# Float64 weights: low words rounded on ScalarE and added as integers, two early units instead of three

## The chip, the cores and the metric

The kernel runs on one core of one Trainium2 chip. The metric is the device time of one execution in microseconds (us), as the median of several runs. A profile of one execution, with its trace, is there beside the times.

## The reference

```python
def _moe2_ref(x, w_in, w_out):          # x: 1152 tokens x 512; w_in 512 x 2048; w_out 2048 x 512
    h = x @ w_in
    relu6 = np.clip(h + 3.0, 0.0, 6.0)
    g = h * relu6 / 6.0
    return (g @ w_out).astype(np.float32)

def reference(...):
    attn_out = _attn_ref(q, k, v)       # windowed attention, 2 x 8 heads x 576 x 64
    x = attn_out -> (1152, 512)
    x = _moe_ref(x, w_gate, w1, w2, capacity)   # top-1 of 8 experts, 512 -> 1024 -> 512
    return _moe2_ref(x, w_in, w_out)    # the dense layer
```

`w_in` and `w_out` are made by dividing a float32 array by a float64 scalar and arrive as float64. The kernel reads them as pairs of 32-bit words, a low and a high one for each number, and has to make float32 of them itself. All else is float32.

## The kernel before, in words

The work has three parts in time: the attention with the routing (to about 80 us), the experts (to about 220 us), and the dense layer. TensorE (PE) multiplies in float32r, with each operand split into a rounded high part and a remainder; a product is three passes (`PASSES`). Splitting a piece of weights of 128x512 takes a ScalarE (ACT) copy at L269 and a VectorE (DVE) subtract at L274, both into a tile named `wt`.

Weights come in units of 256 columns of the hidden dimension. The 32 units of the experts are numbered 0 to 31, the 8 units of the dense layer 32 to 39; a unit has two halves (up and down weights) and four pieces. The halves pass through a ring of 6 raw tiles (`raw`) and a ring of 8 split tiles (`wt`). The dense layer's token groups are 640, 512, then 384 and 256 again; the first group runs over dense units 0 to 3 in eight steps of 128 columns, the second over all eight units. In step f, PE makes the up products (L255 `banks<-x,wt`), then the down products of the step before (L255 `banks<-wt,g`); between them ACT and DVE make the activation: L1558 `r` on ACT, L1561 `gf` on DVE, L1564 `g` on ACT, L1567 `g` on DVE.

A piece of the float64 weights is converted by `conv64`: a load of 128x1024 words into one of three tiles `raw64`; the absolute value of the high word on ACT (L208) into a tile `c64`; then on DVE a clamp (L212), a mask with a shift (L216), a join with the sign (L223), the power of two of the result (L229), the low word multiplied by it (L232), and the add (L238). Tiles `c64` and `t64` have two buffers each.

Dense units 0 to 2 (`NSC = 3`) are converted early, while the experts run: their loads go out on the GpSimd (POOL) queue, their results go from `t64` to DRAM (L241, `wd_dram`) on the same queue, and are loaded back into a raw tile (L1136) on it when the unit is due. Units 3 to 7 are converted straight into their raw tile; their loads go out on the SyncE (SP) queue, after the last load of expert weights.

The order on each engine is written by a planner when the program is built. Jobs (a load, a conversion, a split) are lists of operations with assumed costs for each engine; `fill` puts into the gaps of the engines what fits, in the order of a due time, and `need` forces whatever a unit still lacks. Early conversions have a late due time (`m + ZDUE`, three units after their own), conversions into the raw tile an early one (`m - AHEAD[1]`, 1.5 units before), splits that of their unit. `Ring` keeps when buffers come free in the planner's time. Engines work in the order of the program: an operation that waits holds up all behind it on its engine.

Of the kernel before, what the change touches and what calls it, by code (L numbers as in the profile page):

```python
# [9 lines left out]
F32 = mybir.dt.float32  # L10
# [4 lines left out]
U32 = mybir.dt.uint32  # L15
AF = mybir.ActivationFunctionType
# [7 lines left out]
def tile_kernel(ctx, tc, q, k, v, w_gate, w1, w2, w_in, w_out, out, cap):  # L24
    nc = tc.nc
# [149 lines left out]
    NDU = DFF // FU  # L175
    UW = 2 * NC * FU
    HW = UW // 4
    NSC = 3
    cv = ctx.enter_context(tc.tile_pool(name="cv", bufs=2))
    wd_dram = [dram.tile([128, UW], F32, name=f"wd_dram{u}") for u in range(NSC)]  # L180
    w_in32 = w_in.bitcast(U32)
    w_out32 = w_out.bitcast(U32)
    TINY = 2.0 ** -15
    HUGE = 131071.9921875

    def conv64(u, i, dst):

        box = {}  # L190

        queue = nc.gpsimd if u < NSC else nc.sync

        def load():
            box["raw"] = raw = cv.tile([128, 2 * HW], U32, name="raw64", bufs=NR64)
            if i < 2:
                src = w_in32[256 * i : 256 * i + 256, 2 * FU * u : 2 * FU * u + 2 * FU]
                queue.dma_start(raw.rearrange("p (c f) -> p c f", c=2), src.rearrange("(c p) f -> p c f", p=128))
            else:
                r0 = FU * u + 128 * (i - 2)  # L200
                queue.dma_start(raw, w_out32[r0 : r0 + 128, :])
            w = raw.rearrange("p (n t) -> p n t", t=2)
            box["lo"], box["hi"] = w[:, :, 0], w[:, :, 1]

        def c_abs():
            box["c"] = cv.tile([128, HW], U32, name="c64", bufs=NC64)
            box["t"] = cv.tile([128, HW], F32, name="t64", bufs=NC64)
            nc.scalar.activation(box["c"].bitcast(F32), box["hi"].bitcast(F32), AF.Abs)  # L208

        def c_clamp():  # L210
            c = box["c"].bitcast(F32)
            nc.vector.tensor_scalar(out=c, in0=c, scalar1=TINY, scalar2=HUGE, op0=ALU.max, op1=ALU.min)  # L212

        def c_shift():
            c = box["c"]
            nc.vector.tensor_scalar(  # L216
                out=c, in0=c, scalar1=0x07FFFFFF, scalar2=3, op0=ALU.bitwise_and, op1=ALU.logical_shift_left
            )

        def a_join():  # L220
            d = dst()
            box["a"] = a = box["hi"].bitcast(F32) if d is None else d
            nc.vector.scalar_tensor_tensor(  # L223
                out=a.bitcast(U32), in0=box["hi"], scalar=0xC0000000, in1=box["c"],
                op0=ALU.bitwise_and, op1=ALU.bitwise_or,
            )

        def c_power():
            nc.vector.tensor_single_scalar(box["c"], box["a"].bitcast(U32), 0xFF800000, op=ALU.bitwise_and)  # L229

        def t_low():
            nc.vector.scalar_tensor_tensor(  # L232
                out=box["t"], in0=box["lo"], scalar=2.0 ** -52, in1=box["c"].bitcast(F32), op0=ALU.mult, op1=ALU.mult
            )

        def t_add():
            a, t = box["a"], box["t"]
            nc.vector.tensor_tensor(out=a if u >= NSC else t, in0=a, in1=t, op=ALU.add)  # L238

        def store():  # L240
            nc.gpsimd.dma_start(wd_dram[u][:, HW * i : HW * i + HW], box["t"])  # L241

        return load, c_abs, c_clamp, c_shift, a_join, c_power, t_low, t_add, store

    NR64, NC64 = 3, 2

# [80 lines left out]
    with ExitStack() as actx:  # L329
# [514 lines left out]
        def early_relu(u):  # L844
            def run(e):
                if "hfE" not in box:
                    box["hfE"] = cv.tile([128, HW], F32, name="t64", bufs=NC64)
                    box["hE"] = cv.tile([128, HW], F32, name="t64", bufs=NC64)
                if e == "A":
                    nc.scalar.activation(box["hfE"][:, early_part(u)], box["uE", u], AF.Relu)  # L850
                else:
                    V.tensor_scalar_max(box["hfE"][:, early_part(u)], box["uE", u], 0.0)

            return run
# [245 lines left out]
            self.rel.append(None)  # L1100
            return len(self.rel) - 1

    r_raw, r_wt, r_64, r_ct = Ring(2 * NRAW), Ring(2 * NWT), Ring(NR64), Ring(NC64)

    def whole(m):

# [42 lines left out]
    def conv_job(u, i, m=None):  # L1149
        h = i // 2  # L1150
        ix = {}

        def dst():
            return None if m is None else raw_t[m, h][:, HW * (i % 2) : HW * (i % 2) + HW]

        load, c_abs, *mid, t_add, store = conv64(u, i, dst)

        def gate_load():
            a = 0.0 if m is None or (m, h) in raw_t else r_raw.free(raw_at[m, h])
            b = r_64.free()  # L1160
            return None if a is None or b is None else max(a - 2.0, b)

        def run_load(e, fin):
            if m is not None and (m, h) not in raw_t:
                take_raw(m, h)
            ix["raw"] = r_64.take()
            load()
            return (fin if m is not None else spend("D", 1.46, fin)) + 2.0

        def run_abs(e, fin):  # L1170
            ix["ct"] = r_ct.take()
            c_abs()
            return fin

        def plain(fn):
            def run(e, fin):
                fn()
                return fin + 0.13

            return run  # L1180

        def run_add(e, fin):
            t_add()
            r_64.rel[ix["raw"]] = fin
            if m is not None:
                r_ct.rel[ix["ct"]] = fin
                raw_ready[m, i] = fin + 0.2
            return fin + 0.2

        def run_store(e, fin):  # L1190
            store()
            r_ct.rel[ix["ct"]] = fin + 2.0
            stored[u, h] = stored.get((u, h), 0) + 1
            return fin

        now = lambda: 0.0
        ops = [({"D": 1.46} if m is not None else {"P": 1.1}, gate_load, run_load), ({"A": 0.6}, r_ct.free, run_abs)]
        ops += [({"V": c}, now, plain(fn)) for c, fn in zip((0.34, 0.4, 0.62, 0.34, 0.62), mid)]
        ops.append(({"V": 0.62}, now, run_add))
        return ops + ([({"P": 1.1}, now, run_store)] if m is None else [])  # L1200

    def split_job(m, i):
# [468 lines left out]
    def dense_again():  # L1671

        for t0 in range(0, NTOK, 512):
            n = min(512, NTOK - t0)
            acc = [bank("acc") for _ in range(n // 128)]
            for u in range(DFF // FU):
                halves = [wk.tile([128, 2, NC, 256], F32R, name="xT256", bufs=XTB) for _ in range(2)]
                halves = [x.rearrange("p a c f -> p a (c f)") for x in halves]
                for i in range(NPC):
                    r = wk.tile([128, HW], F32, name="xg", bufs=3)  # L1680
                    if u < NSC:
                        nc.sync.dma_start(r, wd_dram[u][:, HW * i : HW * i + HW])
                    else:
                        load, c_abs, *mid, t_add, _ = conv64(u, i, lambda: r)
                        for fn in (load, c_abs, *mid, t_add):
                            fn()
                    high, low = split_ops(halves[i // 2], r, i % 2)
                    high("A")
                    low()
                for b in range(2):  # L1690
                    ph = bank("rot")[:, 0:n]
                    up = [
                        (w_up(halves, wi, c, 128 * b, 128), x2[:, xi, c, t0 : t0 + n]) for wi, xi in PASSES for c in range(NC)
                    ]
                    mm(ph, up)
                    r = wk.tile([128, 512], F32, name="y", bufs=1)[:, 0:n]
                    gf = wk.tile([128, 2, 256], F32R, name="h", bufs=4).rearrange("p a n -> p (a n)").bitcast(F32)[:, 0:n]
                    g = wk.tile([128, 2, NC, 128], F32R, name="xT128", bufs=XTB).rearrange("p a c t -> p a (c t)")[:, :, 0:n]
                    nc.scalar.activation(r, ph, AF.Relu, bias=c_three)
                    V.scalar_tensor_tensor(out=gf, in0=r, scalar=6.0, in1=ph, op0=ALU.min, op1=ALU.mult)  # L1700
                    nc.scalar.copy(g[:, 0], gf)
                    V.tensor_tensor(out=g[:, 1], in0=gf, in1=g[:, 0].bitcast(F32), op=ALU.subtract)
                    for i in range(n // 128):
                        mm(
                            acc[i],
                            [(g[:, gi, 128 * i : 128 * i + 128], w_dn(halves, wi, b, 0, DM)) for wi, gi in PASSES],
                            start=(u == b == 0), stop=(u == DFF // FU - 1 and b == 1),
                        )
# [165 lines left out]

    est.update(clock)
    est["D"] = max(est["D"], done["rk"] + 1.7)
    for ring, t in ((r_64, est["P"]), (r_ct, done["g0"] + 4.0)):
        ring.rel = [t] * ring.n
    for _ in range(NFIRST):
        assert advance(lambda j, e, t, c: e == "D")  # L1880
# [111 lines left out]
```

## Time and profile before

| what | value |
|---|---|
| median of 3 runs | 438.41 us (437.16 to 441.8) |
| the profiled execution | 438.62 us |
| its span, first to last instruction | 436.9 us |
| mean granted TensorE clock | 0.987 |
| busy in the span | PE 407.5 us, DVE 320.4 us, ACT 225.0 us, POOL 68.2 us |
| chain that ended last, by engine | PE 57%, DVE 20%, DMA 9%, issue 8%, ACT 3% |

Busy time of PE counts matmuls that overlap, so that a stall of PE is read from the starts of its matmuls. The chain is followed back from the last instruction, at each step to what released it.

### The profile page before, as it was taken

The numbers are of one execution on the slowest core, as the hardware profiler recorded it, in microseconds if no ns is written. First come the engines' busy times: TensorE is split into PE (matmuls) and PEld (weight loads), VectorE is DVE, ScalarE is ACT, GpSimd is POOL, SyncE is SP. The second block draws the span as 40 slices with busy tenths as digits, with TensorE's granted clock in tenths as the row PEclk, the third lists the DMA queues.
The fourth block names the chain that finished last, engine by engine and source line by source line (L and its number), as shares of the span: only waits on it lengthen the run. The fifth ranks groups of instructions, "written<-read, shape, count | busy, mean of one in ns | idle before, by whom it ended". The sixth has DMA issues, their size and how long they took to land.

```text
span 436.9 us, 8572 instructions
## 1 busy us (share of the span) xinstructions
PE 407.5 (93%) x3055; PEld 345.8 (79%) x3055; DVE 320.4 (73%) x864; ACT 225.0 (51%) x495; POOL 68.2 (16%) x138
## 2 busy tenths in 40 slices
PE   7999887899999999999999887999999999999990
PEld 4887665597889998978989776888888888999980
DVE  2888967688999999799874899999999323322530
ACT  4786864564668876464761653465554222322320
POOL 8533405024020020212200000000000000200200
PEclk9999999999999999999999998999999999999996
DMA  9997957989999998789914333442410000100110
GB/s 174 202 224 179 302 206 253 362 263 373 372 345 315 312 364 244 251 288 347 344 62 115 94 105 96 146 106 88 145 50 0 1 0 2 72 24 1 53 47 28
DMA packets 68114, 75.98 MB, mean 174 GB/s; under 512 B 31104, under 2 KB 49536, under 8 KB 68064
## 3 DMA queue, kind: packets, MB, share of 16 engines
q1 hardware_dynamic: 62928, 57.70, 43.7%
q0 software_dynamic: 5136, 17.67, 11.4%
q8 instruction: 26, 0.43, 0.4%
q14 instruction: 24, 0.20, 0.1%
HBM read 67.49 MB, written 7.86 MB: 172 GB/s over the span
## 4 chain that ended last, share of the span: by engine, by line
PE 57%; DVE 20%; DMA 9%; issue 8%; ACT 3%; SPq 1%; POOL 0%; POOLq 0%; DVEq 0%; ACTq 0%
PE banks L255 48%; DVE wt L274 7%; DMA raw<-in_moe_w_dram 4%; PE banks L512 2%; PE banks L630 2%; DMA c<-x_dram,sidx 1%; DVE neg L589 1%; DMA v_sb<-in_v_dram 1%; PE banks L1472 1%; PE banks L612 1%; DMA wd_dram<-t 1%; DVE t L232 1%; DVE raw L223 1%; PE banks L576 1%; SPq L480 1%
## 5 line engine op out<-in xcount | busy, mean ns | idle before, releaser
L255 PE MATMUL banks<-x,wt 128*128 128x320 f32 (+3 forms) x576 | 108.6, 340 | 2.5 <-DVE wt L274 2.2
L255 PEld LDWEIGHTS banks<-x,wt 128*128 128x128 f32 x576 | 95.7, 191 | 12.8 <-DVE wt L274 2.7
L255 PE MATMUL banks<-wt,g 128*128 128x512 f32 x384 | 93.9, 392 | 2.9 <-ACT g L1564 1.4
L255 PEld LDWEIGHTS banks<-wt,g 128*128 128x128 f32 x384 | 71.4, 188 | 18.4 <-DVE wt L274 2.1
L274 DVE TENSOR_TENSOR wt<-raw,wt 128x512 fp32r<-128x512 f32 x128 | 82.5, 682 | 3.4 <-ACT wt L269 3.3
L269 ACT CAST wt<-raw 128x512 fp32r<-128x512 f32 x128 | 74.1, 622 | 19.4 <-DMA raw<-wd_dram 7.3
L1561 DVE SCALAR_TENSOR_TENSOR gf<-r,banks 128x320 f32<-128x320 f32 (+3 forms) x48 | 26.5, 552 | 55.1 <-ACT r L1558 55.1
L1558 ACT ACTIVATE r<-banks,c_three 128x320 f32<-128x320 f32 (+3 forms) x48 | 27.9, 580 | 63.8 <-PE banks L255 63.8
L255 PE MATMUL banks<-xT,wt 128*128 128x256 f32 (+2 forms) x288 | 38.7, 283 | 1.0 <-ACT hf L1428 0.7
L255 PEld LDWEIGHTS banks<-xT,wt 128*128 128x128 f32 x288 | 35.0, 191 | 3.1 <-DVE wt L274 0.8
L255 PE MATMUL banks<-h,wt 128*128 128x256 f32 (+2 forms) x288 | 37.0, 279 | 0.0
L255 PEld LDWEIGHTS banks<-h,wt 128*128 128x128 f32 x288 | 34.6, 192 | 0.5 <-issue 0.5
L1564 ACT CAST g<-gf 128x320 fp32r<-128x320 f32 (+2 forms) x40 | 21.4, 536 | 25.4 <-DVE gf L1561 25.3
L208 ACT ACTIVATE c<-raw 128x512 f32<-128x512 f32 x32 | 21.6, 674 | 16.4 <-DVE t L232 13.2
L1567 DVE TENSOR_TENSOR g<-gf,g 128x320 fp32r<-128x320 f32 (+2 forms) x40 | 23.3, 582 | 8.2 <-ACT g L1564 8.1
L1604 POOL DMA_INDIRECT out_dram<-raw,cidx x4 | 4.0, 988 | 142.5 <-ACT raw L1601 134.9
L255 PE MATMUL banks<-wt,xT 128*128 128x256 f32 x144 | 21.6, 293 | 1.3 <-DVE wt L274 0.8
L589 DVE CUSTOM_DVE_ANT_0 neg<-banks,tmask 128x128 f32<-128x128 f32 x72 | 16.2, 284 | 8.8 <-PE banks L576 8.8
L232 DVE SCALAR_TENSOR_TENSOR t<-raw,c 128x512 f32<-128x512 uint32 x32 | 22.0, 688 | 0.6
L602 ACT ACTIVATE pe<-neg,nmx 128x128 f32<-128x128 f32 x72 | 22.3, 392 | 0.1
L223 DVE SCALAR_TENSOR_TENSOR raw<-raw,c 128x512 uint32<-128x512 uint32 x32 | 22.0, 687 | 0.5
L255 PEld LDWEIGHTS banks<-wt,xT 128*128 128x128 f32 x144 | 18.6, 190 | 3.9 <-DVE wt L274 2.3
(288 smaller groups left out, 573.9 us busy)
## 6 DMA issues: line engine op xcount, KB each, us to landing
raw<-in_moe_w_dram SPq DMA_DIRECT2D x64, 512.0 KB, 6.3
raw<-in_moe_w_in_dram SPq DMA_DIRECT2D x10, 512.0 KB, 3.8
raw<-in_moe_w_out_dram SPq DMA_DIRECT2D x10, 512.0 KB, 3.7
early<-in_moe_w_dram SPq DMA_DIRECT2D x8, 512.0 KB, 7.3
raw<-in_moe_w_in_dram POOLq DMA_DIRECT2D x6, 512.0 KB, 7.2
raw<-in_moe_w_out_dram POOLq DMA_DIRECT2D x6, 512.0 KB, 7.0
wd_dram<-t POOLq DMA_DIRECT2D x12, 256.0 KB, 5.9
raw<-wd_dram POOLq DMA_DIRECT2D x6, 512.0 KB, 6.8
```

The costliest lines, as they stand in the source:

```text
L208: nc.scalar.activation(box["c"].bitcast(F32), box["hi"].bitcast(F32), AF.Abs)
L223: nc.vector.scalar_tensor_tensor(out=a.bitcast(U32), in0=box["hi"], scalar=0xC0000000, in1=box["c"], op0=ALU.bitwise_and, op1=ALU.bitwise_or,)
L232: nc.vector.scalar_tensor_tensor(out=box["t"], in0=box["lo"], scalar=2.0 ** -52, in1=box["c"].bitcast(F32), op0=ALU.mult, op1=ALU.mult)
L255: nc.tensor.matmul(out, l, r, start=(start and n == 0), stop=(stop and n == len(pairs) - 1))
L269: nc.scalar.copy(hi, r)
L274: V.tensor_tensor(out=lo, in0=r, in1=hi.bitcast(F32), op=ALU.subtract)
L589: V.tensor_tensor_reduce(out=neg[:, hp, :], in0=box["sp", g][:, hp, :], in1=tmask[:, first, :], scale=-1.0, scalar=3.0e38, op0=ALU.add, op ...
L602: nc.scalar.activation(pe[:, hp, :], neg[:, hp, :], AF.Exp, bias=nmx[:, hp : hp + 1], scale=-1.0)
L1558: nc.scalar.activation(r, ph, AF.Relu, bias=c_three)
L1561: V.scalar_tensor_tensor(out=gf, in0=r, scalar=6.0, in1=ph, op0=ALU.min, op1=ALU.mult)
L1564: nc.scalar.copy(hi, gf)
L1567: V.tensor_tensor(out=lo, in0=gf, in1=hi.bitcast(F32), op=ALU.subtract)
```

## The change

Per piece, ACT gets a second operation: the low word, an unsigned integer, is multiplied by 2^-29 and written back in place as a rounded integer (0 to 8). DVE then joins clamp, shift and sign into `c64` and adds the two words as 32-bit integers: the power of two (L229) and the multiplication of the low word (L232) are gone, and the add has integer operands. The tile `t64` is taken only by the add of an early piece, with a ring of its own, and the planner counts it free 5 us after the store's issue instead of 2. `NSC` goes from 3 to 2, so that dense unit 2 is converted straight into its raw tile. The upper limit of the clamp and the planner's costs change with it.

```diff
-    NSC = 3
+    NSC = 2
...
-    HUGE = 131071.9921875
+    HUGE = 122880.0
...
         def c_abs():
             box["c"] = cv.tile([128, HW], U32, name="c64", bufs=NC64)
-            box["t"] = cv.tile([128, HW], F32, name="t64", bufs=NC64)
             nc.scalar.activation(box["c"].bitcast(F32), box["hi"].bitcast(F32), AF.Abs)
+
+        def c_round():
+            nc.scalar.activation(box["lo"], box["lo"], AF.Copy, scale=2.0 ** -29)
...
         def a_join():
-            d = dst()
-            box["a"] = a = box["hi"].bitcast(F32) if d is None else d
             nc.vector.scalar_tensor_tensor(
-                out=a.bitcast(U32), in0=box["hi"], scalar=0xC0000000, in1=box["c"],
+                out=box["c"], in0=box["hi"], scalar=0xC0000000, in1=box["c"],
                 op0=ALU.bitwise_and, op1=ALU.bitwise_or,
             )
 
-        def c_power():
-            nc.vector.tensor_single_scalar(box["c"], box["a"].bitcast(U32), 0xFF800000, op=ALU.bitwise_and)
-
-        def t_low():
-            nc.vector.scalar_tensor_tensor(
-                out=box["t"], in0=box["lo"], scalar=2.0 ** -52, in1=box["c"].bitcast(F32), op0=ALU.mult, op1=ALU.mult
-            )
-
         def t_add():
-            a, t = box["a"], box["t"]
-            nc.vector.tensor_tensor(out=a if u >= NSC else t, in0=a, in1=t, op=ALU.add)
+            d = dst()
+            if d is None:
+                box["t"] = d = cv.tile([128, HW], F32, name="t64", bufs=NT64)
+            nc.vector.tensor_tensor(out=d.bitcast(U32), in0=box["c"], in1=box["lo"], op=ALU.add)
...
+    NR64, NC64, NT64 = 3, 2, 2
...
         def run_add(e, fin):
+            if m is None:
+                ix["t"] = r_t.take()
             t_add()
-            r_64.rel[ix["raw"]] = fin
+            r_64.rel[ix["raw"]] = r_ct.rel[ix["ct"]] = fin
...
         def run_store(e, fin):
             store()
-            r_ct.rel[ix["ct"]] = fin + 2.0
+            r_t.rel[ix["t"]] = fin + 5.0
...
-        ops += [({"V": c}, now, plain(fn)) for c, fn in zip((0.34, 0.4, 0.62, 0.34, 0.62), mid)]
-        ops.append(({"V": 0.62}, now, run_add))
+        ops.append(({"A": 0.57}, now, plain(c_round)))
+        ops += [({"V": c}, now, plain(fn)) for c, fn in zip((0.34, 0.34, 0.61), mid)]
+        ops.append(({"V": 0.61}, now if m is not None else r_t.free, run_add))
```

## Rows read from the trace of the kernel before

**Rows 1.** Stretches: length, busy us (x count) by engine; TensorE clock, DMA share, GB/s.

```profile
core 0: us, PE busy (x) PEld busy (x) DVE busy (x) ACT busy (x) POOL busy (x), PEclk, DMA share, GB/s
...
134.00:166.00 32.00, 31.23 (x253) 29.92 (x252) 31.26 (x70) 24.60 (x54) 3.70 (x3) 1.00 0.99 332
...
220.00:280.00 60.00, 54.86 (x295) 48.71 (x296) 49.22 (x101) 26.37 (x51) 1.09 (x2) 0.97 0.31 94
280.00:300.00 20.00, 20.00 (x90) 16.57 (x89) 19.59 (x37) 10.58 (x18) 0.00 (x0) 1.00 0.37 107
```

**Rows 2.** The chain that ended last: start, us, what.

```profile
276.83 149.89 PE banks L255 x725
```

**Rows 3.** PE in order of time: start, us, what [idle before <- releaser].

```profile
230.33 3.68 PE L255 MATMUL banks<-x,wt 128*128 128x320 f32 x24
...
237.27 3.68 PE L255 MATMUL banks<-x,wt 128*128 128x320 f32 x24
...
246.30 3.68 PE L255 MATMUL banks<-x,wt 128*128 128x320 f32 x24
...
253.24 3.68 PE L255 MATMUL banks<-x,wt 128*128 128x320 f32 x24
...
261.70 0.74 PE L255 MATMUL banks<-x,wt 128*128 128x320 f32 x4
264.63 4.88 PE L255 MATMUL banks<-x,wt 128*128 128x320 f32 x20 [2.19 <-DVE wt L274]
...
272.77 3.68 PE L255 MATMUL banks<-x,wt 128*128 128x320 f32 x24
...
280.13 2.88 PE L255 MATMUL banks<-x,wt 128*128 128x512 f32 x12
```

**Rows 4.** Waits of PE from 205 to 285: total us, times, longest.

```profile
PE banks L255 <- DVE wt L274: 3.4, 2, 2.2
PE banks L255 <- ACT g L1564: 1.4, 1, 1.4
```

**Rows 5.** The chain, 214 to 242.

```profile
215.50 16.53 issue
232.04 4.67 DMA wd_dram<-t
...
237.23 3.91 DMA raw<-wd_dram
```

**Rows 6.** DVE in order of time.

```profile
231.05 0.69 DVE L238 TENSOR_TENSOR t<-raw,t 128x512 f32<-128x512 f32 x1
...
242.25 0.49 DVE L1561 SCALAR_TENSOR_TENSOR gf<-r,banks 128x320 f32<-128x320 f32 x1 [6.88 <-ACT r L1558]
...
257.66 1.28 DVE L274 TENSOR_TENSOR wt<-raw,wt 128x512 fp32r<-128x512 f32 x2
```

**Rows 7.** Groups by line: count, busy us, mean ns, idle before.

```profile
L232 DVE SCALAR_TENSOR_TENSOR t<-raw,c 128x512 f32<-128x512 uint32 x32 | 22.0, 688 | 0.6
L223 DVE SCALAR_TENSOR_TENSOR raw<-raw,c 128x512 uint32<-128x512 uint32 x32 | 22.0, 687 | 0.5
...
L208 ACT ACTIVATE c<-raw 128x512 f32<-128x512 f32 x32 | 21.6, 674 | 16.4 <-DVE t L232 13.2 <-PE banks L1405 1.3 <-DMA raw<-in_moe_w_out_dram 1.0
...
L238 DVE TENSOR_TENSOR raw<-raw,t 128x512 f32<-128x512 f32 x20 | 13.8, 688 | 0.3
L229 DVE TENSOR_SCALAR c<-raw 128x512 uint32<-128x512 uint32 x32 | 13.7, 429 | 0.6
...
L216 DVE TENSOR_SCALAR c<-c 128x512 uint32<-128x512 uint32 x32 | 13.6, 425 | 0.3
...
L212 DVE TENSOR_SCALAR c<-c 128x512 f32<-128x512 f32 x32 | 13.4, 420 | 2.0 <-ACT c L208 1.9
```

**Rows 8.** Waits of PE from 85 to 205.

```profile
PE banks L255 <- DVE wt L274: 1.0, 4, 0.3
...
PE banks L1308 <- DVE xg L1300: 0.6, 1, 0.6
```

**Rows 9.** Stores to `wd_dram`, L241: us from issue to landing.

```profile
DMA to landing us min/median/max: 2.9/5.9/8.4
```

More of the change, by code (lines that the diff above doesn't have):

```diff
@@ L220, in a_join @@
         def a_join():
-            d = dst()
-            box["a"] = a = box["hi"].bitcast(F32) if d is None else d
             nc.vector.scalar_tensor_tensor(
-                out=a.bitcast(U32), in0=box["hi"], scalar=0xC0000000, in1=box["c"],
+                out=box["c"], in0=box["hi"], scalar=0xC0000000, in1=box["c"],
                 op0=ALU.bitwise_and, op1=ALU.bitwise_or,
             )
-        def c_power():
-            nc.vector.tensor_single_scalar(box["c"], box["a"].bitcast(U32), 0xFF800000, op=ALU.bitwise_and)
-        def t_low():
-            nc.vector.scalar_tensor_tensor(
-                out=box["t"], in0=box["lo"], scalar=2.0 ** -52, in1=box["c"].bitcast(F32), op0=ALU.mult, op1=ALU.mult
-            )
         def t_add():
-            a, t = box["a"], box["t"]
-            nc.vector.tensor_tensor(out=a if u >= NSC else t, in0=a, in1=t, op=ALU.add)
+            d = dst()
+            if d is None:
+                box["t"] = d = cv.tile([128, HW], F32, name="t64", bufs=NT64)
+            nc.vector.tensor_tensor(out=d.bitcast(U32), in0=box["c"], in1=box["lo"], op=ALU.add)
         def store():
             nc.gpsimd.dma_start(wd_dram[u][:, HW * i : HW * i + HW], box["t"])
-        return load, c_abs, c_clamp, c_shift, a_join, c_power, t_low, t_add, store
-    NR64, NC64 = 3, 2
+        return load, c_abs, c_round, c_clamp, c_shift, a_join, t_add, store
+    NR64, NC64, NT64 = 3, 2, 2
     NFU = F // FU
@@ L846, in run @@
                 if "hfE" not in box:
-                    box["hfE"] = cv.tile([128, HW], F32, name="t64", bufs=NC64)
-                    box["hE"] = cv.tile([128, HW], F32, name="t64", bufs=NC64)
+                    box["hfE"] = cv.tile([128, HW], F32, name="t64", bufs=NT64)
+                    box["hE"] = cv.tile([128, HW], F32, name="t64", bufs=NT64)
                 if e == "A":
@@ L1101, in take @@
             return len(self.rel) - 1
-    r_raw, r_wt, r_64, r_ct = Ring(2 * NRAW), Ring(2 * NWT), Ring(NR64), Ring(NC64)
+    r_raw, r_wt, r_64, r_ct, r_t = Ring(2 * NRAW), Ring(2 * NWT), Ring(NR64), Ring(NC64), Ring(NT64)
     def whole(m):
@@ L1154, in dst @@
             return None if m is None else raw_t[m, h][:, HW * (i % 2) : HW * (i % 2) + HW]
-        load, c_abs, *mid, t_add, store = conv64(u, i, dst)
+        load, c_abs, c_round, *mid, t_add, store = conv64(u, i, dst)
         def gate_load():
@@ L1182, in run_add @@
         def run_add(e, fin):
+            if m is None:
+                ix["t"] = r_t.take()
             t_add()
-            r_64.rel[ix["raw"]] = fin
+            r_64.rel[ix["raw"]] = r_ct.rel[ix["ct"]] = fin
             if m is not None:
-                r_ct.rel[ix["ct"]] = fin
                 raw_ready[m, i] = fin + 0.2
@@ L1683, in dense_again @@
                     else:
-                        load, c_abs, *mid, t_add, _ = conv64(u, i, lambda: r)
-                        for fn in (load, c_abs, *mid, t_add):
+                        load, *mid, t_add, _ = conv64(u, i, lambda: r)
+                        for fn in (load, *mid, t_add):
                             fn()
@@ L1876, in tile_kernel @@
     est["D"] = max(est["D"], done["rk"] + 1.7)
-    for ring, t in ((r_64, est["P"]), (r_ct, done["g0"] + 4.0)):
+    for ring, t in ((r_64, est["P"]), (r_ct, done["g0"] + 4.0), (r_t, done["g0"] + 4.0)):
         ring.rel = [t] * ring.n
```

## The prediction

> **What bounds the kernel now.** The chain that ended last says first where nothing can be gained: its last piece of weight is PE alone, 149.89 us without a break from 276.83 on [rows 2]. Whatever the conversions cost after that point, they cost no time, though DVE is busy 19.59 of 20 us there [rows 1]. So a gain has to come from before, and it passes to the end in full, as nothing after 277 waits for anything but PE. The reader is to look for stalls of PE, and the starts of its matmuls show them: the up products of a dense step that nothing disturbs begin 6.94 us after those of the step before (230.33 to 237.27) [rows 3]. The next distances are 9.03 (to 246.30), 6.94 (to 253.24), 8.46 (to 261.70), 11.07 (to 272.77) and 7.36 (to 280.13). Over five times 6.94 that is 2.09 + 0 + 1.52 + 4.13 + 0.42 = 8.16 us lost between 237 and 280. The waits of PE name 4.8 us of it, the low halves of split weights from DVE (3.4) and one activation (1.4) [rows 4]; the rest is matmuls that start slowly behind a stall (20 of them in 4.88 us at 264.63, where 24 take 3.68 otherwise) [rows 3].
>
> Two causes lie behind these 8.16 us. The first is a trip through DRAM: the last add of unit 2 ends near 231.7 [rows 6], its store lands 4.67 us after 232.04 and its reload 3.91 us after 237.23 [rows 5]. ACT stands with a copy of that raw tile at its head, and DVE idles 6.88 us until 242.25 behind ACT [rows 6]. The second is DVE itself: from 242 on it works off the conversions of units 3 and 4 that were held up, and the low halves of unit 2, which are behind them in the order, come at 257.66 [rows 6], one PE stall later. Within 220 to 280 DVE is busy 49.22 of 60 us [rows 1]; without the idle 6.88 that is 93% of what is left.
>
> While the experts run, PE hardly stops, though DVE is full (31.26 of 32 us between 134 and 166) [rows 1]: PE's waits for DVE from 85 to 205 are 1.0 us in four and 0.6 in one [rows 8].
>
> **The operations of a piece.** Removed from DVE: the power (0.429 us) and the low product (0.688), 1.117 us a piece; clamp 0.420, mask with shift 0.425, join 0.687 and the add stay [rows 7]. The add of integers isn't in the trace; between 0.425, the cheapest operation of this size, and twice the float add (1.38) I take the float add's 0.688, the same sizes and two inputs [rows 7]. So a piece takes 2.220 us of DVE instead of 3.337. Over the program: 32 pieces by 1.117 = 35.7 us less DVE.
>
> Added to ACT: a rounding of 128x512 in place, integer in and out with a stride of two words, 32 of them. The nearest row is the absolute value, which reads with that stride: 0.674 us [rows 7]. The bounds are 0 in time, if it falls into idle time, and twice 0.674, if integers or the strided write halve the rate. An added operation can't gain. I take 0.674, 21.6 us in all. From 220 to 280 ACT is busy 26.37 of 60 us [rows 1]; some 12 pieces add 8.1 us (16.2 at the upper bound), so it stays below three quarters, and I charge nothing. The cover is ACT's idle 33.6 us; without it each rounding would hold the copies and activations queued behind it for 0.674 us, 8.1 us in the stretch.
>
> *A rule that speaks against this part:* DVE does such an operation of one input in 0.425 us, ACT in 0.674 [rows 7]. The Trainium skill, in "ScalarE: Activation LUTs", Rules for kernel authors, says that additions, multiplications and the like belong on VectorE and not on ScalarE. The per-operation rows agree with that, and by it the rounding should be a DVE operation: the saving would shrink from 35.7 to 35.7 - 32 x 0.425 = 22.1 us of DVE. The stretch decides otherwise: there DVE is the engine that is short and ACT is not.
>
> **Unit 2 converted late.** Early pieces go from 12 to 8: while the experts run DVE has 12 x 3.337 = 40.0 us of conversion before and 8 x 2.220 = 17.8 after, 22.3 less; in the dense layer 20 x 3.337 = 66.7 before and 24 x 2.220 = 53.3 after, 13.4 less. POOL loses four loads, four stores and two reloads, and DMA 2 MB (4 stores of 256 KB, 2 reloads of 512 KB). SP gets the four loads. They stand behind the last expert load, as unit 3's did, so what is queued behind them is unit 3's loads alone, which wait for the same three `raw64` tiles. The DRAM trip of unit 2 is gone, and with it ACT's block and DVE's 6.88 us.
>
> Does DVE manage the dense layer's start? The up products at 230.33 belong to step 2, so at PE's full pace unit 3's up weights are due in step 6, four times 6.94 later, at 258.1 [rows 3]. From 220 until then, 38.1 us, DVE has two `gf` and two `g` for each of six steps (24 by some 0.48, the first of them in rows 6: 11.5 us), about 13 splits by 0.64 (half of the 1.28 at 257.66 [rows 6]: 8.3), and six pieces of units 2 and 3 (13.3): 33.1 us. If the planner also puts unit 4's four pieces in front, as their due times allow, it is 42.0, or 3.9 too much. Some of unit 2's work can move ahead of 220, where early pieces are gone. So it fits, without much to spare. I take 7.2 of the 8.16 us as gained and leave 1 us, two stalls like the 0.42 us at 272.77 [rows 3]; what is late next is the low halves of unit 3.
>
> **While the experts run.** 22.3 us less DVE work, and 2 MB less traffic. PE's waits for DVE add up to 1.6 us in the rows named [rows 8], and about as much again goes to matmuls that start slowly behind them, as at 264.63: 3 us at most. A new order removes some and makes others; I take 1.5 (bounds: 3 gained, 2 lost).
>
> **A new wait.** The add of an early piece waits for `t64`, that is for the store of the piece two before. Behind it on DVE stand the splits of the experts. Stores land 2.9 to 8.4 us after their issue, 5.9 in the middle [rows 9], and the planner counts 5. With eight early pieces over some 100 us the tile should be free; I charge nothing.
>
> **The sum**, against the profiled execution: 438.62 - 7.2 - 1.5 = 429.9. That execution lies 0.2 above the median shown, so 429.7 us. Clamp limit and planner costs change no duration; the planner's new costs are part of the new order.
>
> **The rivals.**
> - *The stall is half kept.* The planner puts unit 4's conversions and unit 2's in front of the splits that PE waits for, as it did before 257.66. For it: 42.0 us of work in 38.1; against it: a piece costs DVE a third less than when that order came out so. 3.9 of the 8.16 us stay, and the experts give 1: 438.6 - 4.3 - 1 = 433.3.
> - *The gain goes to ACT or another trip.* By the page cited above ACT is the wrong place. As a mechanism here: roundings stand in front of the activations that PE waits for (1.4 us already [rows 4]), 12 by 0.674 = 8.1 us, which eats the gain: about 437. The same time comes out if the change doesn't do what it says, because the low-priority stores of unit 1 are now the late ones and their trip (4.67 + 3.91 us) stalls the same engines.
> - *Slower: the add waits for the store.* Where POOL is held by a gather, the store goes out late, and DVE stands in the full stretch (31.26 of 32 us) up to 8.4 us [rows 9] with splits behind it. The gain of 8.7 us is lost from the second such wait on, if nothing hides it: two of the middle length (11.8) give 441.7, two of the longest 446.7. Against it: eight early pieces over some 100 us are 12 us apart on average.
> - *More than that:* all stalls of both stretches go: 438.6 - 8.2 - 3 = 427.4, and the lighter traffic may take waits for expert weights too, to 425.
>
> **How the numbers follow.** Forecast (427.5 to 432) 0.55; more (425 to 427.5) 0.12; half kept (432 to 436) 0.16; ACT or another trip (436 to 441) 0.09; slower 0.08, nearly all above 441. The range from 425 to 436.5 holds 0.83 or so. The bounds of the unknown costs lie within it: a rounding at twice 0.674 is still covered, and an integer add at 1.38 costs DVE 0.69 on six pieces, 4.2 us, which gives the half-kept case. One per cent, 4.4 us, is about what a measurement of this kernel can tell from no change. Below 434.0: 0.55 + 0.12 + half of 0.16 and a little, 0.77; within 1%: 0.16; slower by more: 0.07.
>
> **What would show it.** In the profile after: no `wd_dram` reload on the chain near 237, no idle of DVE near 235 to 242; distances of up products of 6.94 us from 230 to the end of the first group; L229 and L232 gone, the add at 0.69 and the rounding near 0.67 us; the unbroken piece of PE at the chain's end beginning some 8 us earlier, and still some 150 us long. It would be wrong if PE waits for `wt` as long as before in that stretch, if waits of L238's successor for a DMA appear on DVE, or if the experts' part, to the first dense matmul, ends later than 219.

## The result and the profile after

The changed kernel takes 434.44 us (median of 11 runs, 432.86 to 438.08), the kernel before, run beside it, 439.26; the ratio is 0.990, with a 95% interval of 0.9875 to 0.9932. So it is faster by about 1%, 4.3 us by the ratio (4.8 by the medians), half of the 8.7 that the sum gave and 4.7 us above the forecast, though inside the range. Medians are of all executions; ratios, here and below, leave out those that took over 1.5% longer than the fastest of their kernel, so a ratio need not be the quotient of two medians. The profiled execution took 434.86 us against 438.62, its span is 432.9 us, the mean granted clock 0.992.

The parts of the profile, in the order of the prediction's own steps. Each operation costs what the sum took. Groups by line of the kernel after, answering [rows 7]:

```profile
L223 DVE SCALAR_TENSOR_TENSOR c<-raw,c 128x512 uint32<-128x512 uint32 x32 | 22.0, 686 | 0.4
...
L210 ACT ACTIVATE raw<-raw 128x512 uint32<-128x512 uint32 x32 | 21.6, 674 | 0.0
...
L232 DVE CUSTOM_DVE_ANT_0 raw<-raw,c 128x1024 uint16<-128x1024 uint16 x24 | 16.5, 687 | 0.8
```

The rounding (L210) takes 674 ns, the integer add (L232) 687; L229 and L232 of before are gone.

The dense layer's start, PE in order of time, answering [rows 3]:

```profile
222.21 0.56 PE L249 MATMUL banks<-x,wt 128*128 128x320 f32 x2
...
233.42 3.68 PE L249 MATMUL banks<-x,wt 128*128 128x320 f32 x24
...
240.36 3.68 PE L249 MATMUL banks<-x,wt 128*128 128x320 f32 x24
...
247.30 0.74 PE L249 MATMUL banks<-x,wt 128*128 128x320 f32 x4
248.90 3.51 PE L249 MATMUL banks<-x,wt 128*128 128x320 f32 x20 [0.86 <-DVE wt L268]
...
255.67 3.68 PE L249 MATMUL banks<-x,wt 128*128 128x320 f32 x24
...
262.61 1.04 PE L249 MATMUL banks<-x,wt 128*128 128x320 f32 x6
264.15 2.90 PE L249 MATMUL banks<-x,wt 128*128 128x320 f32 x18 [0.50 <-DVE wt L268]
...
270.32 3.68 PE L249 MATMUL banks<-x,wt 128*128 128x320 f32 x24
...
277.26 2.88 PE L249 MATMUL banks<-x,wt 128*128 128x512 f32 x12
```

The distances are 6.94, 6.94, 8.37, 6.94, 7.71 and 6.94, so 1.43 + 0.77 = 2.20 us are lost instead of 8.16, both behind low halves of split weights. From the first dense matmul (222.21; 219.13 before) to the second group (277.26; 280.13 [rows 3]) it is 55.05 us against 61.00: 5.95 gained. What follows is as long as it was. The chain that ended last closes with PE alone, answering [rows 2]; it now begins at the last stall, 264.15, and ends at 423.86, where that of before ended at 426.72:

```profile
264.15 159.71 PE banks L249 x783
```

But the first dense matmul comes 3.08 us *later*. 0.75 of it is there before the first matmul on expert weights (84.99 against 84.24). The other 2.33 us are lost while the experts run, 137.22 us (222.21 - 84.99) instead of 134.89 (219.13 - 84.24). The 0.75 is made up at once, since in the kernel before PE waits 0.68 us for an activation at 87.74, and in the changed one it doesn't: at 106.28 both make the same matmul at the same time, as rows below show. Waits of PE from 85 to 205, answering [rows 8]:

```profile
PE banks L249 <- DVE wt L268: 2.5, 3, 1.2
PE banks L1468 <- DMA raw<-in_moe_w_dram: 1.1, 1, 1.1
```

A wait for a transfer of expert weights is new, and the waits for the low halves from DVE have grown from 1.0 to 2.5. The balance of the profiled executions: +0.75 + 2.33 - 5.95 gives -2.87 at PE's last matmul; another 1.14 lie between there and the end of the span (9.04 us against 10.18), where nothing was changed.

Two things stand behind the loss. The first is the add that waits for a store. DVE in order of time:

```profile
102.28 0.68 DVE L223 SCALAR_TENSOR_TENSOR c<-raw,c 128x512 uint32<-128x512 uint32 x1
105.83 0.69 DVE L232 CUSTOM_DVE_ANT_0 t<-raw,c 128x1024 uint16<-128x1024 uint16 x1 [2.87 <-DMA wd_dram<-t]
...
107.50 2.49 DVE L268 TENSOR_TENSOR wt<-raw,wt 128x512 fp32r<-128x512 f32 x4
```

The splits at 107.50 stand behind it, and PE waits for them at 108.24. The second is the stretch around it. PE in order of time, before:

```profile
106.28 0.71 PE L255 MATMUL banks<-wt,xT 128*128 128x256 f32 x4
107.24 1.57 PE L255 MATMUL banks<-wt,xT 128*128 128x256 f32 x8 [0.24 <-DVE wt L274]
...
113.53 1.09 PE L1472 MATMUL banks<-raw,xT 128*64 128x128 f32 x16
...
121.46 1.04 PE L1472 MATMUL banks<-raw,xT 128*64 128x128 f32 x16
```

After:

```profile
106.28 0.71 PE L249 MATMUL banks<-wt,xT 128*128 128x256 f32 x4
108.24 1.58 PE L249 MATMUL banks<-wt,xT 128*128 128x256 f32 x8 [1.25 <-DVE wt L268]
...
115.69 1.09 PE L1468 MATMUL banks<-raw,xT 128*64 128x128 f32 x16 [1.08 <-DMA raw<-in_moe_w_dram]
...
123.00 1.58 PE L249 MATMUL banks<-wt,xT 128*128 128x256 f32 x8 [0.92 <-DVE wt L268]
...
125.43 1.04 PE L1468 MATMUL banks<-raw,xT 128*64 128x128 f32 x16
```

The same matmuls come 1.00 us later at 108.24, 2.16 at 115.69 and 3.97 at 125.43, so more than the whole loss lies in these 19 us; 0.89 us of it come back later. The chain there:

```profile
100.60 12.88 DMA raw<-in_moe_w_dram
```

This load of expert weights needed 12.88 us to land. How the 16 DMA engines are shared from 97 to 123 us shows in the view of transfers. Its lines give packets, MB and share of each queue (q1 is SP's, q0 POOL's), then for a kind of transfer the number, the KB of one and the median us to landing. Before:

```profile
q1 hardware_dynamic: 5185, 6.82, 76.0%
q0 software_dynamic: 795, 2.75, 28.2%
...
raw<-in_moe_w_dram SPq DMA_DIRECT2D x13, 512.0 KB, 7.4
```

After:

```profile
q1 hardware_dynamic: 4928, 6.41, 72.7%
q0 software_dynamic: 898, 3.12, 31.9%
...
raw<-in_moe_w_dram SPq DMA_DIRECT2D x9, 512.0 KB, 9.0
```

The engines were full in both (the two shares add up to 104%). Early pieces that are ready sooner send 0.37 MB more through POOL's queue in these 26 us (five stores and four early loads go out there, against three and three); 9 loads of expert weights go out instead of 13, and each takes longer.

### The profile page after: what moved, and what is told of

The parts are those of the page before. It is cut to its first block, busy times and chain, and to the rows that moved or that the text cites. A ratio compares the mean times of both kernels' runs of the same rounds, so it can differ in the third digit from the quotient of the medians.

```text
span 432.9 us, 8533 instructions
## 1 busy us (share of the span) xinstructions
PE 406.1 (94%) x3055; PEld 345.4 (80%) x3055; DVE 290.0 (67%) x800; ACT 241.4 (56%) x527; POOL 62.5 (14%) x128
## 4 chain that ended last, share of the span: by engine, by line
PE 65%; DVE 14%; DMA 10%; ACT 5%; issue 3%; POOL 0%; POOLq 0%; ACTq 0%; DVEq 0%; SPq 0%
PE banks L249 52%; DVE wt L268 4%; DMA raw<-in_moe_w_dram 4%; PE banks L506 2%; DMA c<-x_dram,eI 2%; PE banks L624 2%; DMA c<-x_dram,sidx 1%; PE banks L1493 1%; PE banks L1468 1%; PE banks L570 1%; PE banks L606 1%; DVE c L223 1%; DVE g L1563 1%; PE banks L663 1%; ACT wt L263 1%
## 5 line engine op out<-in xcount | busy, mean ns | idle before, releaser
L249 PE MATMUL banks<-x,wt 128*128 128x320 f32 (+3 forms) x576 | 107.4, 337 | 1.8 <-DVE wt L268 1.4
L249 PEld LDWEIGHTS banks<-x,wt 128*128 128x128 f32 x576 | 94.3, 188 | 12.2 <-DVE wt L268 2.2
L249 PE MATMUL banks<-wt,g 128*128 128x512 f32 x384 | 92.8, 390 | 0.0
L223 DVE SCALAR_TENSOR_TENSOR c<-raw,c 128x512 uint32<-128x512 uint32 x32 | 22.0, 686 | 0.4
L210 ACT ACTIVATE raw<-raw 128x512 uint32<-128x512 uint32 x32 | 21.6, 674 | 0.0
```

The source lines that it names most:

```text
L210: nc.scalar.activation(box["lo"], box["lo"], AF.Copy, scale=2.0 ** -29)
L223: nc.vector.scalar_tensor_tensor(out=box["c"], in0=box["hi"], scalar=0xC0000000, in1=box["c"], op0=ALU.bitwise_and, op1=ALU.bitwise_or,)
L249: nc.tensor.matmul(out, l, r, start=(start and n == 0), stop=(stop and n == len(pairs) - 1))
```

## The experiments

Theory A: early pieces finish sooner, so that an add waits for its store and their transfers crowd out the experts' loads. Theory B: the roundings on ACT stand in front of the splits. For each kernel the table gives its early pieces; "experts", from the first matmul on expert weights to the first dense one; "stretch", within them, from the second to the fourth group of 16 matmuls on `raw` and `xT` (100.86 to 121.46 before), which doesn't depend on when the experts begin; "dense start", from the first dense matmul to the second group; all from PE's rows of its one profile. The ratio comes from timed runs beside the kernel before, whose median was 438.10 to 439.53 us in the several sets, so that kernels are compared by their ratios. A stage of one profile and the timed runs can differ by 2 to 4 us, so verdicts rest on stalls that have a row and on ratios.

| kernel | early pieces | experts | stretch | dense start | median | ratio (95%) |
|---|---|---|---|---|---|---|
| before | 12 | 134.89 | 20.60 | 61.00 | 439.26 | 1 |
| after | 8 | 137.22 | 24.57 | 55.05 | 434.44 | 0.990 (0.9875, 0.9932) |
| arith_only | 12 | 139.58 | 22.86 | 52.85 | 436.62 | 0.994 (0.9911, 0.9973) |
| late_only | 8 | 133.69 | 20.61 | 62.84 | 438.24 | 0.999 (0.9962, 1.0017) |
| wait9 | 8 | 138.98 | 25.76 | 54.95 | 436.44 | 0.990 (0.9859, 0.9938) |
| hold120 | 8 | 137.66 | 20.60 | 54.91 | 435.39 | 0.991 (0.9883, 0.9945) |
| hold4_120 | 8 | 138.62 | 21.83 | 54.83 | 435.62 | 0.995 (0.9920, 0.9973) |
| nsc1 | 4 | 132.97 | 21.77 | 63.14 | 438.73 | 0.999 (0.9961, 1.0021) |
| round_twice | 8 | 139.05 | 24.33 | 53.43 | 437.04 | 0.997 (0.9940, 0.9991) |
| extra_traffic | 8 | 140.37 | 28.05 | 55.05 | 437.28 | 0.998 (0.9950, 1.0015) |
| one_ring | 8 | 136.78 | 23.25 | 55.94 | 435.41 | 0.991 (0.9882, 0.9945) |
| sp_early | 8 | 140.94 | 27.01 | 55.36 | 438.16 | 0.998 (0.9950, 1.0007) |
| one_ring_sp | 8 | 142.20 | 29.69 | 56.08 | 439.52 | 1.001 (0.9976, 1.0047) |
| ring_hold140 | 8 | 138.86 | 20.60 | 56.25 | 437.17 | 0.994 (0.9896, 0.9973) |
| ring_nsc1 | 4 | 132.26 | 20.61 | 67.14 | 439.21 | 0.999 (0.9957, 1.0018) |
| ring_hold160 | 8 | 131.99 | 20.59 | 55.68 | 429.99 | 0.978 (0.9731, 0.9834) |

**One part alone.** `arith_only` is the changed kernel with three early units, `late_only` the kernel before with two.

```diff
-    NSC = 2
+    NSC = 3
```

> The change's arithmetic with three early units as before (NSC = 3). Theory A (the dense start gained from two causes, DVE work and the DRAM trip of unit 2; the experts lost by early pieces that come sooner, through a store that DVE waits for and through crowded DMA): the order of the first pieces is that of the changed kernel, so the experts lose the same 2 to 3 us, the trip is earlier but still there, and the dense start keeps 2 to 5 of its 8.2 us: 435 to 438. Theory B (the experts lose because the roundings stand in front of the splits on ACT): twelve roundings instead of eight, a loss of 3 to 4 us there, 436 to 439. What the arithmetic alone gives in the dense start is read from the distances of the up products.

> The old arithmetic with unit 2 converted late (NSC = 2 in the kernel before). Theory A: early pieces are as slow as before, so nothing is lost while the experts run (first dense matmul near 219); no DRAM trip at the dense start, but six pieces more of 3.337 us there, 39.8 us of DVE work in 38.1: about half of the 8.2 us stays, 434 to 437. Theory B: no roundings, so the same for the experts. If the time is that of the changed kernel or below, the arithmetic is worth nothing.

The arithmetic alone takes *all* stalls out of the dense start, where theory A had it keep 2 to 5 of its 8.2 us. PE in order of time, `arith_only`:

```profile
238.78 3.68 PE L249 MATMUL banks<-x,wt 128*128 128x320 f32 x24
...
245.72 3.68 PE L249 MATMUL banks<-x,wt 128*128 128x320 f32 x24
...
252.66 3.68 PE L249 MATMUL banks<-x,wt 128*128 128x320 f32 x24
...
259.60 3.68 PE L249 MATMUL banks<-x,wt 128*128 128x320 f32 x24
```

Every distance is 6.94, with unit 2 still going through DRAM: its trip is no longer late. Its last store goes out at 200.54, 27.0 us before the first dense matmul, where that of before went out 12.9 us behind it (232.04). Two early units without the arithmetic give a longer dense start, 62.84 us, in which DVE is busy 61.09 of 64 us (221 to 285), and no gain in time, where theory A expected 434 to 437 us. So the gain there belongs to the shorter piece on DVE; the later conversion gives a little of it back (four pieces more, 2.20 us of stalls). While the experts run fewer early pieces go with shorter times (139.58 to 137.22, and 134.89 to 133.69), differences that single profiles don't show for certain. In the stretch the kernel with two early units and the old arithmetic loses nothing (20.61 us).

**The wait and the order.** `wait9` has the planner count a store 9 us instead of 5. `hold120` has the planner hold all early loads until 120 us of its time, `hold4_120` all but the first four (with `NR64 + 4`).

```diff
             b = r_64.free()
+            if m is None and b is not None and len(r_64.rel) >= NR64:
+                b = max(b, HOLD)
```

> The changed kernel, with the planner counting the tile t64 free 9 us after the store's issue instead of 5, so that the add is put later in DVE's order. Theory A: DVE's wait of 2.87 us for a store near 103 to 106 goes, and with it the 1.4 us stall of PE near 108; the crowded DMA stays: 1 us less, 433 to 434. Theory B: no difference, 434.4.

> The changed kernel, with all early loads held until 120 us in the planner's time, behind the stretch in which the weights of experts land late. Theory A: expert weights land within 8 us as before, no DVE wait for a store, and the 2.5 to 3 us lost while the experts run come back, the first dense matmul near 219: 430.5 to 432. Theory B: the roundings only come later, the loss stays: 434 to 435. If a store is now so late that a reload waits for it, the trip shows again at the dense start, up to 3 us.

> The changed kernel, but only the first four of the eight early pieces may be loaded before the planner's 120 us; the other four wait until then. Theory A (the early pieces come sooner, so one add waits for its store and the loads meet the experts' weights between 97 and 123 us): the about 2.8 us lost between 101 and 123 us against the kernel before go down to under 1 us, and since the other four are done well before 190 us they do not collide at the experts' end as with all eight held (2.8 us lost at 193 to 206). Experts (first matmul on expert weights to first dense matmul) 134.5 to 136 us against 137.2 of the changed kernel, dense start 54.9 as before, whole 431 to 433.5 us, ratio to before 0.982 to 0.988. Theory B (the roundings on ScalarE stand in front of the splits of the experts' high words): the roundings are all still there, so the experts stay at 136.5 to 138 us and the time at 434 to 435.5.

In `wait9` the add no longer waits, but a load takes 15.12 us from 98.31 on, and PE waits 3.0 us behind it: the profile's experts are longer, the time is that of the changed kernel. `hold120` has none of these stalls between 97 and 123 (its stretch is 20.60 us, as before), though three of its loads still went out at 88.76 to 90.25; but PE waits for splits near the experts' end, where the held pieces now lie (0.98 us at 203.97), so that the forecast of theory A, 430.5 to 432, was missed too. `hold4_120` missed what it was made for: a hold in the plan is only a place in POOL's order, and with nothing in front of them that waits, three of the second unit's loads went out at 106 to 108 us. The store was waited for as before (2.8 us).

**Doses.** `round_twice` doubles the suspected cost on ACT (the second rounding changes the numbers), `extra_traffic` the traffic.

```diff
+        def c_again():
+            nc.scalar.activation(box["lo"], box["lo"], AF.Copy, scale=1.0)
...
+                if u < NSC:
+                    nc.gpsimd.dma_start(junk[u, i], src)
```

> The changed kernel with every low word rounded twice on ScalarE; the second rounding changes the numbers (it leaves out nothing and its result is wrong in the low bits), and adds 32 times 0.674 us, 21.6 us, of ScalarE. Theory A: ScalarE has room; the second rounding also makes each early piece 0.7 us later, which if anything eases the crowd. Experts 136 to 138 us, dense start 55 to 56, whole 434 to 436.5, ratio to the changed kernel 1.000 to 1.004. Theory B: the first rounding cost the experts some 2.5 us, so the second costs as much again: experts 139 to 140, dense start 55 to 58, whole 437 to 440.

> The changed kernel with one more transfer beside each early load of the up weights (four in all, 2 MB, from DRAM to a DRAM tile that nothing reads, on GpSimd's queue); no instruction of VectorE or ScalarE is added. Theory A: the experts' weight loads that are in flight with them land 2 to 6 us later than in the changed kernel (12.6 to 13.6 us there), and the experts take 1.5 to 5 us longer: 139 to 142 us; dense start unchanged at 55; whole 436 to 440. Theory B: transfers cost nothing here as long as the engines are the limit: experts 137 to 138 us, whole 434 to 436.

`extra_traffic` came out as theory A had it. PE in order of time:

```profile
120.58 1.98 PE L1471 MATMUL banks<-raw,xT 128*64 128x128 f32 x16 [3.56 <-DMA raw<-in_moe_w_dram]
```

The load behind this took 15.95 us, and nothing but transfers was added: bytes on POOL's queue in this stretch are paid for in landings of expert weights. `round_twice` came out at theory B's lower end, but for the dense start, which both put too long. Its rows show a path of both. ACT in order of time:

```profile
104.83 0.67 ACT L207 ACTIVATE c<-raw 128x512 f32<-128x512 f32 x1 [3.21 <-DMA raw<-in_moe_w_out_dram]
105.40 0.67 ACT L210 ACTIVATE raw<-raw 128x512 uint32<-128x512 uint32 x1
106.10 0.68 ACT L213 ACTIVATE raw<-raw 128x512 uint32<-128x512 uint32 x1
106.68 0.36 ACT L1365 ACTIVATE h<-banks 128x256 fp32r<-128x256 f32 x1
106.94 1.12 ACT L266 CAST wt<-raw 128x512 fp32r<-128x512 f32 x2
```

An early load lands late, ACT stands 3.21 us with its absolute value at the head, and the roundings lengthen the line before the split; PE waits 1.73 us for that split at 107.60. ACT is not free where it waits for a transfer. The first rounding alone isn't what the stretch loses, as the last kernel below shows with all its roundings in place. In the dense start even the second one is covered: ACT is busy 46.83 of 55 us there (222 to 277), and no time is lost (53.43 us).

**Fewer early pieces, no store to wait for, one queue.** `nsc1` converts one unit early. `one_ring` adds in place, stores from `c64` and gives that ring all four tiles. `sp_early` sends early loads through SP's queue; `one_ring_sp` does both.

```diff
-                box["t"] = d = cv.tile([128, HW], F32, name="t64", bufs=NT64)
+                box["t"] = d = box["c"].bitcast(F32)
...
-    NR64, NC64, NT64 = 3, 2, 2
+    NR64, NC64 = 3, 4
...
-        queue = nc.gpsimd if u < NSC else nc.sync
+        queue = nc.sync
```

> The changed kernel with one dense unit converted early instead of two: four early pieces, one reload of four pieces; two units are converted in the dense stage. Theory A: with four pieces fewer beside the experts' loads, the experts take 134 to 135.5 us, as short as in the kernel before or the one with the late unit alone. Theory B gives about the same there, 135 to 136.5, since the roundings go too. The dense start pays: four more conversions at 2.22 us of VectorE each, 8.9 us, in a stage where unit 2's conversion already costs 2.2 us of stalls: 57 to 63 us against 55.05. Whole 434 to 440 us. If the dense start stays at 55 us, VectorE was not what its stalls were made of.

> The changed kernel, but an early piece is added in place (its sum overwrites the exponent tile, as the low-word product was overwritten in the kernel before) and stored from there; the two 4 KB tiles of the separate ring join the other ring, which has four. No add can wait for a store any more; nothing else changes but the order that the planner makes of it. Theory A1 (of the experts' loss of 2.3 to 3.1 us about 1 us is the add that waits 2.9 us for its store at 103 us): that wait is gone, the loss between 101 and 109 us falls from 1.0 to under 0.2 us; the loads crowded by early transfers stay. Experts 136 to 137, dense start 53 to 55, whole 432.5 to 434.5, ratio to before 0.984 to 0.990. Theory A2 (the pieces then come sooner still and crowd the loads more): experts 137.5 to 139, whole 434.5 to 437.

> The changed kernel with the eight early loads on SP's queue, in line with the experts' loads, instead of GpSimd's; the bytes are the same. Theory C (the experts' loads land late because transfers of a second queue are served beside them): their landings fall from 12 to 14 us to 7 to 10, the two stalls of PE for a raw tile (1.1 us at 115.7, 1.1 us at 123) go, experts 135 to 136.5 us, whole 432 to 433.5. Theory D (the bytes are what is late, whoever asks for them): the same waits, or waits for an early load that stands in the line before them: experts 137 to 140 us, whole 434 to 437. Dense start 55 in both.

> Both edits: add in place with one ring of four, early loads on SP's queue. If both theories A1 and C hold the experts are as short as in the kernel before, 134.5 to 135.5 us, the dense start 53 to 55, and the whole 430.5 to 432.5 us, ratio to before 0.980 to 0.985. If only one holds, 432.5 to 434. If neither, 434 to 437.

With four early pieces the experts are 4.3 us shorter than with eight, and the dense start pays 8.1 for it. In `one_ring` the add's wait is gone, but the load of raw weights is waited for longer, 1.9 us at 114.89 instead of 1.08, and the time doesn't move (0.991). `sp_early` speaks against theory C, that a second queue is the trouble. PE there:

```profile
113.68 2.60 PE L249 MATMUL banks<-wt,xT 128*128 128x256 f32 x10 [5.54 <-ACT wt L263]
```

The load behind it went out at 100.69 and landed 12.30 us later: in one line early loads stand in front. `one_ring_sp`, with both edits, is the slowest (1.001): PE waits 7.1 us for a split at 112.76, more than "neither holds" allowed for. The Trainium skill, "DMA: Bandwidth & Descriptors", Issuing engines are not separate DMA queues, says that DMAs from SP, ACT and POOL use the same 16 engines. This run agrees: with the early loads on SP's queue the engines are still 0.95 busy from 97 to 123 us (1.05 in the changed kernel), and loads of expert weights take 9.9 us (median; 9.0 there).

**Other places for the second unit.** Left open was whether the second unit's pieces cost what they cost anywhere, or only among these loads. `ring_hold140` and `ring_hold160` are `one_ring` with the second unit's four loads held in the plan until 140 and 160 us, where POOL's order has gathers that wait in front of them. `ring_nsc1` is `one_ring` with one early unit.

```diff
+            if m is None and b is not None and len(r_64.rel) >= NR64 + 4:
+                b = max(b, 160.0)
```

> Added in place with one ring of four, and the second unit's four early loads are held in the planner until 160 us; in GpSimd's order they then stand behind the experts' last gather, which went out at about 161 us. Theory E (the loss is the second four's transfers meeting the experts' loads at 97 to 130 us, where the DMA engines are full; from 169 to 205 us they were 0.9, 0.5 and 0.7 busy): the experts lose nothing before 160 us and at most 1.5 us after: 132 to 134.5 us against 134.9 of the kernel before and 137.2 of the changed one; dense start 55 to 57; whole 428.5 to 432, ratio to before 0.976 to 0.985. Theory F (the pieces cost what they cost wherever they lie, or a unit so late is not stored in time for its reload): experts 136 to 139, or the dense start over 58; whole 434 to 438.

> As the one before with 140 us: the four loads stand behind the gathers of about 131 us. Between 133 and 169 us the DMA engines of the changed kernel were 0.9 to 1.06 busy, so theory E expects some of the crowd there: experts 133.5 to 136 us, dense start 55 to 56, whole 430 to 434. Theory F: 136 to 139 and 434 to 437.

> Added in place with one ring of four, and only one unit early. With the add's wait gone (1.2 us at 101 to 109 us in the kernel with one early unit) and no second four, theory E expects the shortest experts of all, 131.5 to 132.5 us, and the long dense start of that kernel, 62 to 64 us; whole 435 to 438. Theory F expects about the 132.97 us that the kernel with one early unit had.

In `ring_hold160` the loads go out from 164.75 on, and the transfers from 97 to 123 read:

```profile
q1 hardware_dynamic: 5515, 7.20, 83.5%
q0 software_dynamic: 461, 1.47, 16.5%
...
raw<-in_moe_w_dram SPq DMA_DIRECT2D x13, 512.0 KB, 7.3
```

13 loads of 7.3 us, as before. All waits of PE from 85 to 222:

```profile
PE banks L249 <- ACT wt L263: 0.6, 1, 0.6
PE banks L249 <- DVE wt L268: 0.5, 2, 0.2
PE banks L249 <- ACT x L1385: 0.4, 1, 0.4
```

The experts take 131.99 us, 5.2 less than in the changed kernel with the same eight pieces, the dense start 55.68, and the kernel 429.99 us (six executions): 0.978 of before, faster than both, as the intervals don't overlap. At 140 us the stretch is free too (20.60 us), but three of the four loads (133.96 to 135.43) meet expert loads again: PE waits 2.51 us at 151.55 behind a load of expert weights that took 8.27, and experts and time (138.86 and 437.17 us) come out at the upper end of theory F's range, not in E's. `ring_nsc1` has the experts of a program with four pieces (132.26) and a dense start that is longer than theory E had it (67.14).

All kernels whose early loads go out on POOL's queue can be put side by side by what that queue moves from 97 to 123 us. At 0.02 MB (`hold120`) a load of expert weights lands in 5.7 us (median); at 1.25 to 2.75 MB (six kernels, the one before among them) in 6.2 to 7.4; at 2.82 to 4.21 MB (seven, the changed one among them) in 8.9 to 10.8. The stretch takes 20.59 to 20.61 us in the first seven kernels, but for `nsc1`, and 21.83 to 28.05 in the others. `nsc1` has 21.77, with an add that waits 3.0 us for its store; `ring_nsc1`, where it can't, has 20.61. By this pair the add's wait is worth some 1.2 us of the stretch, and the crowd the rest of the 3.97. So the place is what costs, not the pieces. What the hold at 160 us gives without the sum in place was not run.

## Why the prediction was half right

- *What bounds the kernel.* Right: nothing after the first group changed, and a gain ahead of it passed through in full.
- *The operations of a piece.* Right: 0.687 for the add where 0.688 was taken, 0.674 for the rounding where 0.674 was taken. That the rounding lies beside other work holds for the dense start and, as `ring_hold160` shows, for the experts; a second one is covered in the dense start, but no longer among the experts. The rule of the Trainium skill weighed there ("ScalarE: Activation LUTs", Rules for kernel authors) did not decide the time: with all 32 roundings on ACT `ring_hold160` takes 0.978 of the time of before. But no run has the rounding on DVE, so that what the rule advises stays untested.
- *Unit 2 converted late.* 7.2 of 8.16 us were taken, 5.95 came. The stall is 2.20 us instead of 1, and what is late is the low halves, as forecast. But the working put half of it down to the DRAM trip that the late conversion removes. `arith_only` keeps the trip's transfers and loses nothing; `late_only` removes them, with four more pieces of 3.337 us on DVE in the stage, and gains nothing. DVE's time a piece was enough to make all of the loss, and the trip was late because DVE was.
- *While the experts run*: this step failed. The working took 1.5 us gained, with 2 lost as the worst; 2.33 were lost over the stage and 3.97 in the stretch from 106 to 125 us alone. It counted DVE time saved and 2 MB less traffic over the whole stage. It didn't ask what the quicker pieces would start sooner: their stores and next loads move into 97 to 123 us, where the DMA engines were full before the change.
- *A new wait*: this failed in its size. "I charge nothing", with eight pieces "12 us apart on average"; in fact three stores went out within 8 us (99.01, 101.60 and 106.81), one add waited 2.87 us and PE 1.25. Taking this wait away alone gave no time back (`wait9`, `one_ring`); the crowd behind it remained.
- *The rivals.* The time is near that of "the stall is half kept" (433.3), but not by its mechanism: most of the stall went, and the experts took back part of the gain. That the time lies inside the stated range is luck to that extent. The slower rival named the right place, the add behind its store, at too high a price: one wait, not two or more.
- Two of the tests named for being wrong are what the profile shows: experts that end later than 219 (222.21), and an early piece's add on DVE that waits for a DMA (2.87 us).

What stays open: why the same stretch gives waits of 1 us in one order and of 3 in another (`wait9` against `one_ring`); each new order moves some load, and no single one was isolated.

## What to carry to other kernels

When a filler job gets cheaper, ask what it will start sooner: its buffers come free earlier, and its transfers move to where it can least be used. Read the DMA share of each stretch before counting bytes over a stage; here 0.37 MB more in 26 full microseconds went with 3.97 us lost there, and 2 MB less overall did not make up for it. A hold in a planner's time is only a place in an engine's order, and it holds an operation back only if something in front of it waits.

## What was not expected of the hardware

The integer add of 128x512 words is recorded as a custom operation on 128x1024 uint16 and takes 0.687 us, as long as the float add (0.688 [rows 7]).

The granted clock can dip in the routing part, which puts off the first matmul on expert weights; the executions of one kernel spread over some 5 us, of which this may be a part. PE in order of time, `one_ring` and then `ring_hold160`, which run the same matmuls there:

```profile
79.83 0.63 PE L1303 MATMUL banks<-ident,xg 128*128 128x128 f32 x4 [1.65 <-issue]
80.29 1.88 PE L249 MATMUL banks<-early,c 128*128 128x512 f32 x4
...
84.33 2.00 PE L249 MATMUL banks<-wt,xT 128*128 128x256 f32 x12
```

```profile
80.96 0.73 PE L1305 MATMUL banks<-ident,xg 128*128 128x128 f32 x4 [2.66 <-issue]
81.49 3.51 PE L249 MATMUL banks<-early,c 128*128 128x512 f32 x4
...
87.16 1.99 PE L249 MATMUL banks<-wt,xT 128*128 128x256 f32 x12
```

After an idle time of 1.65 us the four matmuls take 1.88 us, after one of 2.66 they take 3.51: the clock went to its lower level, 1.2 instead of 2.4 GHz, and the mean granted clock from 80 to 84 us is 0.67 against 1.00. The first matmul on expert weights comes 2.83 us later, 1.13 of it from the later start at 80.96 and 1.70 from there on. The length of the idle time alone doesn't settle it: after 2.26 us in `hold4_120` and 2.35 in `ring_hold140` the clock stayed at 1.00, after 2.28 in `wait9` it dipped. Six other profiles have 0.57 to 0.70 in these 4 us and begin the experts between 85.79 and 87.99; the nine with 1.00 begin them between 84.05 and 85.36. A stall while the experts run can have the same price on top: behind the 3.56 us in `extra_traffic` 16 matmuls take 1.98 us (granted clock 0.80 from 121 to 133), where those at 115.69 of the changed kernel, behind 1.08, take 1.09.
